# A scan inside groups of 8 tokens: a tree up and down around the levels over groups, for serial steps and a wide product

## The chip, the cores and the metric

The kernel runs on one core of a Trainium2 chip. The metric is device time in microseconds of one execution; a comparison is made from several executions of each kernel on the same chip. The clock that the profile grants TensorE is given as a share of its higher level (1.00 is 2.4 GHz, 0.50 is 1.2 GHz).

## What is computed

A linear attention with a complex decay, then two feed-forward layers. Cut to what matters:

```python
# q, k, v, a_re, a_im: (4, 8, 768, 48) float32
mag = sqrt(a_re**2 + a_im**2)
a = (a_re + 1j * a_im) * minimum(mag, 0.999) / (mag + 1e-6)
for t in range(768):                       # per batch and head
    S = a[t][:, None] * S + outer(k[t], v[t])
    y[t] = q[t] @ S.real
x = y.transpose(0, 2, 1, 3).reshape(3072, 384)
h = maximum(x @ w_in, 0);  x = (h * h) @ w_out        # 384 -> 2048 -> 384
h = x @ w2_in;  out = (h * sigmoid(1.702 * h)) @ w2_out
```

The kernel doesn't step through t. Inside a stretch of tokens it needs the running products of the decays a from the stretch's start, for every token; q is multiplied by them and k by their inverse, and the rest is matrix products with a causal mask.

## The kernel before

**Units and chunks.** The 3072 tokens are cut into twelve units of 256 tokens (three per batch), and each unit into two chunks of 128. A unit's tokens lie in 32 groups of J = 8 consecutive tokens. In the tile `ab` of a unit (128 partitions x 2 x 8 x 96) the two planes c are the real and the imaginary part, j is the token within its group of 8, and the last axis is 3 blocks of 32 groups.

**What a unit does, in order.** `normalize(u)` (line 414) loads the decays, transposes them (line 405) and scales them (up to line 448). `scan(u)` (line 454) makes the running products: first seven serial steps over j, each multiplying plane j by plane j-1 (one multiply into `mm`, line 467, and a difference and a sum, lines 471 and 473); after them plane 7 holds the product of each group. Then five levels over the 32 groups of plane 7 (lines 491 and 495, doubling the stretch each time) make running products of groups. ScalarE copies these, shifted by one group, to `eexc` with a 1 ahead of each block, and their negated imaginary part (lines 505 and 506). At last planes 0 to 6 are multiplied by the product of all groups before theirs, in two halves of four and three planes: two multiplies and a sum each (lines 514 and 518). Behind the scan, q and k are multiplied (lines 529 and 571), written to `scr` in device memory (lines 535 and 585), and read back with heads turned as `qs` (line 599; for the first two chunks half of the loads are issued on ScalarE's queue).

**What a chunk does.** `chunk` (line 621) makes scores on TensorE (`pa`, line 638), masks them on GpSimd (`asb`, line 642), multiplies them by v (`px`), and carries the state. Its result is the input `xh`, `xl` of the first layer.

**The layers.** Work on the layers comes in jobs: twelve of 256 tokens for the first, then eight of 384 for the second, each of sixteen steps m over the 2048 hidden columns. A step has a first product (`h`, line 837) and a second (`acc`, lines 882 and 884). Weights arrive as packed words: `decode` (line 738) loads one to a `raw` buffer (of three, line 742), and ScalarE (lines 750, 753) and VectorE (lines 755, 756, 758) make `wf` of it; `split` (line 764) makes a high and a low part (line 779 on ScalarE, line 780 on VectorE) for the three-term products. Job 0 uses unsplit first weights and jobs 0 to 2 unsplit second ones. `wf`, high and low parts live in a ring `w` of 66 slots; for the first eight steps of the second layer, high and low parts live in the buffers that the attention no longer needs. A job's end is three evictions (`o`, line 894) and stores to `x2d` (line 895).

**What sets the order.** All of this is first noted as operations with an engine, an assumed duration, the buffers that they read and write, and due times. `Plan` then simulates the engines: at each moment it gives an engine the operation that can start earliest, and among those the most urgent, so an engine whose urgent operation isn't ready takes any other that is. It does this forty times, moving due times earlier where TensorE stood idle, and emits the order with the earliest end. Each engine, and SyncE's queue of loads, then runs its list in that order. Buffers are rings: the next buffer of a ring is given out in the order of the program and only when a slot is free.

Of the kernel before, what the change touches and what calls it, by code (L numbers as in the profile page):

```python
# [24 lines left out]
J = 8  # L25
# [9 lines left out]
BLAME = 1.5  # L35

# [24 lines left out]

class Op:
    __slots__ = ("eng", "ns", "lat", "fn", "due", "prio", "pred", "raw", "succ", "bufs", "wait", "start", "end", "idx", "ready", "port", "fresh")


class Plan:
# [5 lines left out]
    PORT = ()  # L72
    AHEAD = {"PE": 0, "DVE": 0, "ACT": 0, "POOL": 0, "SP": 0}
# [13 lines left out]
    def op(self, eng, ns, fn, r=(), w=(), lat=None, due=1e12, port=True):  # L87
        o = Op()
        o.eng, o.ns, o.fn, o.due, o.port = eng, float(ns), fn, due, port and eng in self.PORT
# [52 lines left out]
    def forward(self):  # L142
# [15 lines left out]
        order, freed, held = [], [], dict.fromkeys(self.PORT, 0.0)  # L158
# [20 lines left out]
        while len(order) < len(ops):  # L179
            best = None  # L180
            for e in sorted(cand, key=free.get):
# [4 lines left out]
                for o in os:  # L186
                    t = earliest(o)
                    if t is None:
                        continue
                    t = max(t, f)  # L190
                    if o.port:
                        t = max(t, held["POOL" if e == "DVE" else "DVE"])
                    can.append((t, o.prio, o.idx, o))
# [3 lines left out]
                urgent = min((c for c in can if c[0] <= pick[0] + self.AHEAD[e]), key=lambda c: c[1:3])  # L197
# [10 lines left out]
            if o.port:  # L208
                held[o.eng] = t + o.ns
# [37 lines left out]
def fast(ctx: ExitStack, tc: tile.TileContext, q, k, v, a_re, a_im, w1, w2, out, flag):  # L247
# [47 lines left out]
    ring("m", 1)  # L295
# [7 lines left out]
    ring("w", 4 * NF + 2)  # L303
# [35 lines left out]
    eexc = const.tile([128, 3, 3, 32], F32, name="eexc")  # L339
# [4 lines left out]
    def setup():  # L344
        def consts():
            P.memset(tiny, 2.0 ** -56)
            P.memset(shb, SH * math.log(2.0))
            P.memset(eexc, 0.0)
            P.memset(eexc[:, 0, :, 0:1], 1.0)
# [10 lines left out]
        op("POOL", 800, consts, w=["consts", "eexc", "eexm"])  # L360
# [42 lines left out]
    def tr(u, dst, nm, w):  # L403
        t = nat_t.pop((u, nm))
        op("DVE", ve(96 * groups(u)), lambda: V.transpose(out=f(dst()), in_=t().rearrange("p h j d -> p j h d")), r=[t], w=w, port=False)
# [5 lines left out]
    def planes(ab, js, cs=(0, 1)):  # L411
        return [(ab, c, j) for c in cs for j in range(js.start, js.stop)]

    def normalize(u):
        J = groups(u)
        ab = ab_t[u] = buf("ab", [128, 2, J, 96], name="ab")
# [37 lines left out]
    def scan(u):  # L454
        J, CPU = groups(u), count(u)
        HJ, U = (J + 1) // 2, 32 * J
        ab = ab_t.pop(u)
        load_nat(u, "q", q)
        load_nat(u, "k", k)

        for j in range(1, J):
            m = buf("mm", [128, 2, 2, 96], name="mm")

            def go(j=j, m=m):
                x = ab()[:, :, j - 1].unsqueeze(1).to_broadcast([128, 2, 2, 96])
                y = ab()[:, :, j].unsqueeze(2).to_broadcast([128, 2, 2, 96])
                V.tensor_tensor(m(), x, y, ALU.mult)  # L467

            js = slice(j, j + 1)
            op("DVE", ve(384), go, r=planes(ab, slice(j - 1, j + 1)), w=[m])  # L470
            op("DVE", ve(96), lambda j=j, m=m: V.tensor_tensor(ab()[:, 0, j], m()[:, 0, 0], m()[:, 1, 1], ALU.subtract),
               r=[m], w=planes(ab, js, (0,)))
            op("DVE", ve(96), lambda j=j, m=m: V.tensor_tensor(ab()[:, 1, j], m()[:, 0, 1], m()[:, 1, 0], ALU.add),
               r=[m], w=planes(ab, js, (1,)))
# [3 lines left out]
        while h < 32:  # L478
# [10 lines left out]
            def times(c, parts=parts):  # L489
# [7 lines left out]
            for c in range(2):  # L497
                op("DVE", ve(96), lambda c=c, times=times: times(c), r=lastp, w=[(m, c)])
# [5 lines left out]
        g = lambda: ab()[:, :, J - 1].rearrange("p c (x r) -> p c x r", r=32)  # L504
        op("ACT", 240, lambda: A.copy(eexc[:, 0:2, :, 1:32], g()[:, :, :, 0:31]), r=lastp, w=["eexc"])
        op("ACT", 170, lambda: A.mul(eexc[:, 2, :, 1:32], g()[:, 1, :, 0:31], -1.0), r=[lastp[1]], w=["eexm"])
# [655 lines left out]
```

## Time and profile before

| | before |
|---|---|
| runs, median of 3 | 1070.24 us (1068.86 to 1072.58) |
| profiled execution | 1070.3 us |
| its span, first to last instruction | 1068.6 us |
| TensorE busy | 968.2 us |
| VectorE busy | 751.9 us |
| ScalarE busy | 608.3 us |
| GpSimd busy | 48.6 us |

Time outside the span is 1.7 us. In the rows below PE is TensorE (PEld its weight loads), DVE is VectorE, ACT is ScalarE, POOL is GpSimd and SP is SyncE; a q behind a name is the engine's queue, as it issues transfers. L467 is line 467 of the kernel. `out<-in` are tile names, and x is a count.

### The profile page before, as it was taken

The numbers are of one execution on the slowest core, as the hardware profiler recorded it, in microseconds if no ns is written. First come the engines' busy times: TensorE is split into PE (matmuls) and PEld (weight loads), VectorE is DVE, ScalarE is ACT, GpSimd is POOL, SyncE is SP. The second block draws the span as 40 slices with busy tenths as digits, with TensorE's granted clock in tenths as the row PEclk, the third lists the DMA queues.
The fourth block names the chain that finished last, engine by engine and source line by source line (L and its number), as shares of the span: only waits on it lengthen the run. The fifth ranks groups of instructions, "written<-read, shape, count | busy, mean of one in ns | idle before, by whom it ended". The sixth has DMA issues, their size and how long they took to land.

```text
span 1068.6 us, 20733 instructions
## 1 busy us (share of the span) xinstructions
PE 968.2 (91%) x7858; PEld 937.7 (88%) x7858; DVE 751.9 (70%) x1514; ACT 608.3 (57%) x1506; POOL 48.6 (5%) x70
## 2 busy tenths in 40 slices
PE   0029899999999999999999999999999999999996
PEld 0028789898999999999999999999999999999996
DVE  6979899899988899998899678843434333333332
ACT  4527587558576666758676799643434333333332
POOL 1000000000101011010100100000000000000000
PEclk9999999999999999999999999999999999999999
DMA  7586867366473637355552754110101010100000
GB/s 206 153 195 164 191 162 144 90 134 146 100 168 81 158 79 142 99 119 142 104 127 62 168 189 141 60 46 1 45 1 45 1 45 4 42 1 23 9 15 26
DMA packets 133486, 102.28 MB, mean 96 GB/s; under 512 B 46848, under 2 KB 125184, under 8 KB 133376
## 3 DMA queue, kind: packets, MB, share of 16 engines
q1 hardware_dynamic: 132000, 99.47, 39.2%
q10 hardware_dynamic: 1376, 1.38, 0.5%
q8 instruction: 64, 1.05, 0.4%
q14 instruction: 46, 0.38, 0.1%
HBM read 72.43 MB, written 28.39 MB: 94 GB/s over the span
## 4 chain that ended last, share of the span: by engine, by line
PE 57%; DVE 22%; DMA 8%; ACT 8%; issue 4%; SPq 1%; DVEq 0%; ACTq 0%
PE h L837 27%; PE acc L884 19%; PE acc L882 10%; DMA x2d<-o 3%; DVE mm L491 2%; DMA raw<-in_w_dram 2%; DVE mm L467 2%; DVE ab L495 2%; DVE gl L852 2%; DVE ab L514 1%; DVE ab L518 1%; DVE wf L756 1%; DVE m L514 1%; DVE wf L758 1%; PE pa L638 1%
## 5 line engine op out<-in xcount | busy, mean ns | idle before, releaser
L852 DVE TENSOR_TENSOR gl<-g,gh 128x256 fp32r<-128x256 f32 (+1 forms) x272 | 132.2, 489 | 96.9 <-ACT gh L851 73.4
L846 DVE TENSOR_TENSOR g<-g,h 128x384 f32<-128x384 f32 x128 | 70.8, 553 | 146.7 <-ACT g L845 146.6
L851 ACT CAST gh<-g 128x256 fp32r<-128x256 f32 (+1 forms) x272 | 124.2, 458 | 78.0 <-DVE g L846 75.2
L845 ACT ACTIVATE g<-h 128x384 f32<-128x384 f32 x128 | 62.9, 491 | 158.8 <-PE h L837 158.8
L837 PE MATMUL h<-xh,wh 128*128 128x256 f32 (+1 forms) x720 | 140.1, 303 | 2.3 <-ACT xh L697 1.1
L837 PE MATMUL h<-xh,wl 128*128 128x256 f32 (+1 forms) x720 | 134.6, 295 | 0.1
L837 PE MATMUL h<-xl,wh 128*128 128x256 f32 (+1 forms) x720 | 134.2, 296 | 0.0
L638 PE MATMUL pa<-qs 96*128 96x128 f32 x384 | 50.6, 285 | 75.1 <-DMA qs<-scr 73.6
L837 PEld LDWEIGHTS h<-xh,wh 128*128 128x128 f32 x720 | 109.4, 188 | 6.6 <-ACT g L842 3.6
L638 PEld LDWEIGHTS pa<-qs 96*128 96x128 f32 x384 | 47.0, 197 | 76.0 <-issue 73.5
L837 PEld LDWEIGHTS h<-xl,wh 128*128 128x128 f32 x720 | 107.9, 188 | 1.7 <-issue 1.1
L842 ACT ACTIVATE g<-h 128x256 f32<-128x256 f32 x192 | 72.8, 382 | 64.2 <-PE h L837 61.2
L837 PEld LDWEIGHTS h<-xh,wl 128*128 128x128 f32 x720 | 108.5, 188 | 0.8 <-DVE wl L780 0.5
L882 PE MATMUL acc<-gh,wh 128*128 128x256 f32 x432 | 80.9, 282 | 7.6 <-ACT o L894 7.5
L843 ACT ACTIVATE g<-g 128x256 f32<-128x256 f32 x192 | 80.0, 420 | 3.5
L882 PE MATMUL acc<-gl,wh 128*128 128x256 f32 x432 | 80.8, 282 | 0.4 <-DVE gl L852 0.2
L884 PE MATMUL acc<-w,gh 128*128 128x384 f32 x384 | 79.7, 336 | 0.0
L882 PE MATMUL acc<-gh,wl 128*128 128x256 f32 x432 | 79.5, 279 | 0.0
L837 PE MATMUL h<-xh,w 128*128 128x384 f32 x384 | 77.7, 337 | 0.1
L882 PEld LDWEIGHTS acc<-gh,wh 128*128 128x128 f32 x432 | 63.1, 189 | 10.1 <-ACT o L894 8.9
L642 POOL TENSOR_SCALAR_AFFINE_SELECT asb<-asb 128x512 f32<-128x512 f32 x48 | 45.2, 950 | 565.8 <-ACT asb L646 565.3
L882 PE MATMUL acc<-g,wf 128*128 128x256 f32 x288 | 69.2, 380 | 0.0
(122 smaller groups left out, 1936.2 us busy)
## 6 DMA issues: line engine op xcount, KB each, us to landing
raw<-in_w_dram SPq DMA_DIRECT2D x64, 384.0 KB
scr<-tq SPq DMA_DIRECT2D x24, 384.0 KB
qs<-scr SPq DMA_DIRECT2D x46, 129.0 KB
qs<-scr SPq DMA_DIRECT2D x46, 128.0 KB
scr<-tk SPq DMA_DIRECT2D x12, 390.0 KB
nat_k<-in_k_dram SPq DMA_DIRECT2D x48, 96.0 KB
scr<-tk SPq DMA_DIRECT2D x12, 384.0 KB
x2d<-o SPq DMA_DIRECT2D x36, 128.0 KB
```

The lines of the kernel that those rows point to most:

```text
L467: V.tensor_tensor(m(), x, y, ALU.mult)
L638: T.matmul(pa()[:, h], lhsT=qs()[:, 4 * g + h, kcol], rhs=qs()[:, 4 * g + h, qcol], start=True, stop=True)
L642: P.affine_select(out=tj, in_=tj, pattern=[[0, 4], [1, J], [J, C // J]], base=0, channel_multiplier=-1, compare_op=ALU.is_ge, fill=0.0)
L837: T.matmul(h()[:, :n], lhsT=ww()[:, kk * 128:kk * 128 + 128], rhs=xx()[:, kk, :n], start=(i == kk == 0), stop=(i == len(terms) - 1 and kk ...
L842: op("ACT", ac(n) - 30, lambda: A.activation(g()[:, :n], h()[:, :n], AF.Relu), r=[h], w=[g])
L843: op("ACT", ac(n), lambda: A.activation(g()[:, :n], g()[:, :n], AF.Square), r=[g], w=[g])
L845: op("ACT", ac(n) - 30, lambda: A.activation(g()[:, :n], h()[:, :n], AF.Sigmoid, scale=1.702), r=[h], w=[g])
L846: op("DVE", ve(n), lambda: V.tensor_tensor(g()[:, :n], g()[:, :n], h()[:, :n], ALU.mult), r=[h, g], w=[g], port=False)
L851: op("ACT", ac(n), lambda: A.copy(gh()[:, :n], g()[:, :n]), r=[g], w=[gh])
L852: op("DVE", ve(n), lambda: V.tensor_tensor(gl()[:, :n], g()[:, :n], gh()[:, :n].bitcast(F32), ALU.subtract), r=[g, gh], w=[gl])
L882: T.matmul(acc[i]()[:, :n], lhsT=ww()[:, i * 128:i * 128 + 128], rhs=gg()[:, :n], **st_)
L884: T.matmul(acc[i](), lhsT=gg()[:, i * 128:i * 128 + 128], rhs=ww(), **st_)
```

## The change

Within a group of 8 tokens the seven serial steps and the wide product are replaced by one tree. The tile gains a plane in front (index 0), so a token's plane j is now index j+1. On the way up, products of neighbours are made for 4, then 2, then 1 planes at once, so that index 8 holds the group's product. The five levels over the 32 groups stay. ScalarE then copies index 8, shifted by one group, to index 0, with a 1 ahead of each block. On the way down, for 1, then 2, then 4 planes at once, a plane is multiplied by the one half a stretch before it. Each such call is two multiplies (one per plane c), a difference and a sum.

`mm` grows from 384 elements per partition to 1536, `ab` by a ninth, the ring `m` goes, and `w` has 65 slots instead of 66. The other edits change nothing that runs: `port`, `PORT` and `held` were empty, and `FILL` and `HOLD` with `HOLD = 0` leave the look-ahead at nought.

```diff
-    ring("m", 1)
-    ring("w", 4 * NF + 2)
+    ring("w", 4 * NF + 1)
-    eexc = const.tile([128, 3, 3, 32], F32, name="eexc")
+    ones2 = const.tile([128, 6], F32, name="ones2")
...
-        ab = ab_t[u] = buf("ab", [128, 2, J, 96], name="ab")
+        full = ab_t[u] = buf("ab", [128, 2, J + 1, 96], name="ab")
+        ab = Part(full, lambda t: t[:, :, 1:])
...
-        for j in range(1, J):
-            m = buf("mm", [128, 2, 2, 96], name="mm")
-            def go(j=j, m=m):
-                x = ab()[:, :, j - 1].unsqueeze(1).to_broadcast([128, 2, 2, 96])
-                y = ab()[:, :, j].unsqueeze(2).to_broadcast([128, 2, 2, 96])
-                V.tensor_tensor(m(), x, y, ALU.mult)
-            js = slice(j, j + 1)
-            op("DVE", ve(384), go, r=planes(ab, slice(j - 1, j + 1)), w=[m])
-            op("DVE", ve(96), lambda j=j, m=m: V.tensor_tensor(ab()[:, 0, j], m()[:, 0, 0], m()[:, 1, 1], ALU.subtract), ...
-            op("DVE", ve(96), lambda j=j, m=m: V.tensor_tensor(ab()[:, 1, j], m()[:, 0, 1], m()[:, 1, 0], ALU.add), ...
+        def times(x, y, n, step):
+            m = buf("mm", [128, 2, 2, n, 96], name="mm")
+            at = lambda k: slice(k, k + (n - 1) * step + 1, step)
+            xs = [(full, c, x + i * step - 1) for c in range(2) for i in range(n)]
+            ys = [[(full, c, y + i * step - 1) for i in range(n)] for c in range(2)]
+            def part(c):
+                V.tensor_tensor(m()[:, c], full()[:, :, at(x)],
+                                full()[:, c:c + 1, at(y)].to_broadcast([128, 2, n, 96]), ALU.mult)
+            for c in range(2):
+                op("DVE", ve(192 * n), lambda c=c: part(c), r=[*xs, *ys[c]], w=[(m, c)])
+            op("DVE", ve(96 * n), lambda: V.tensor_tensor(full()[:, 0, at(y)], m()[:, 0, 0], m()[:, 1, 1], ALU.subtract),
+               r=[(m, 0), (m, 1)], w=ys[0])
+            op("DVE", ve(96 * n), lambda: V.tensor_tensor(full()[:, 1, at(y)], m()[:, 0, 1], m()[:, 1, 0], ALU.add),
+               r=[(m, 0), (m, 1)], w=ys[1])
+        n = J // 2
+        while n:
+            times(J // (2 * n), J // n, n, J // n)
+            n //= 2
...
-        op("ACT", 240, lambda: A.copy(eexc[:, 0:2, :, 1:32], g()[:, :, :, 0:31]), r=lastp, w=["eexc"])
-        op("ACT", 170, lambda: A.mul(eexc[:, 2, :, 1:32], g()[:, 1, :, 0:31], -1.0), r=[lastp[1]], w=["eexm"])
-        ee = eexc.rearrange("p c x r -> p c (x r)")
-        for js in (slice(0, HJ), slice(HJ, J - 1)) if J > 4 else (slice(0, J - 1),):
...
-            op("DVE", ve(192 * n), lambda p2=p2, n=n, mul=mul: mul(p2()[:, :, :n], 1), ...
-            op("DVE", ve(192 * n), lambda js=js, mul=mul: mul(ab()[:, :, js], 0), ...
-            op("DVE", ve(192 * n), lambda p2=p2, js=js, n=n: V.tensor_tensor(
-                ab()[:, :, js], ab()[:, :, js], p2()[:, ::-1, :n], ALU.add), ...
+        def before():
+            g = full().rearrange("p c j (x r) -> p c j x r", r=32)
+            A.copy(g[:, :, 0, :, 1:32], g[:, :, J, :, 0:31])
+        op("ACT", 75, lambda: A.copy(full().rearrange("p c j (x r) -> p c j x r", r=32)[:, :, 0, :, 0],
+                                     ones2.rearrange("p (c x) -> p c x", c=2)), r=["ones2", *lastp], w=[(full, "one")])
+        op("ACT", 240, before, r=[*lastp, (full, "one")], w=first)
+        n = 1
+        while n < J:
+            times(0, J // (2 * n), n, J // n)
+            n *= 2
```

## Rows read from the trace of the kernel before

**Rows 1.** The page's first part: busy us, share of the span, instructions.
```profile
PE 968.2 (91%) x7858; PEld 937.7 (88%) x7858; DVE 751.9 (70%) x1514; ACT 608.3 (57%) x1506; POOL 48.6 (5%) x70
```
**Rows 2.** Busy time by stage: stretch, length, then PE, PEld, DVE, ACT, POOL; clock, DMA.
```profile
0.00:59.00 59.00, 0.00 (x0) 0.00 (x0) 48.90 (x103) 30.38 (x72) 3.40 (x22) 1.00 0.63 174
59.00:88.00 29.00, 14.20 (x177) 12.65 (x178) 22.93 (x62) 9.98 (x27) 3.34 (x4) 1.00 0.90 210
...
133.00:657.00 524.00, 510.21 (x5165) 488.08 (x5158) 472.12 (x962) 379.41 (x995) 39.97 (x42) 1.00 0.56 127
657.00:1068.60 411.60, 402.77 (x2311) 401.84 (x2310) 167.57 (x316) 159.98 (x337) 0.00 (x0) 1.00 0.10 29
```
**Rows 3.** What PE waited for: us in total, times, longest us.
```profile
PE pa L638 <- DMA qs<-scr: 73.6, 3, 72.6
PE acc L882 <- ACT o L894: 7.5, 5, 2.0
...
PE px L671 <- POOL asb L642: 0.5, 2, 0.4
```
**Rows 4.** DVE in order of time, unit 0's serial steps: start us, us, instruction.
```profile
21.98 0.52 DVE L467 TENSOR_TENSOR mm<-ab 128x384 f32<-128x384 f32 x1
22.53 0.26 DVE L471 TENSOR_TENSOR ab<-mm 128x96 f32<-128x96 f32 x1
22.71 0.25 DVE L473 TENSOR_TENSOR ab<-mm 128x96 f32<-128x96 f32 x1
...
25.94 0.55 DVE L467 TENSOR_TENSOR mm<-ab 128x384 f32<-128x384 f32 x1
26.41 0.35 DVE L755 TENSOR_SCALAR wf<-wf 128x384 int32<-128x384 int32 x1
...
31.98 0.25 DVE L473 TENSOR_TENSOR ab<-mm 128x96 f32<-128x96 f32 x1
```
**Rows 5.** DVE in order of time, first and last instruction of unit 0's wide product.
```profile
39.92 0.95 DVE L514 TENSOR_TENSOR m<-ab,eexc 128x768 f32<-128x768 f32 x1
...
45.19 0.75 DVE L518 TENSOR_TENSOR ab<-ab,m 128x576 f32<-128x576 f32 x1
```
**Rows 6.** ACT by line: count, busy us, mean ns, idle before and its releaser.
```profile
L505 ACT COPY eexc<-ab 128x186 f32<-128x186 f32 x12 | 4.1, 346 | 10.6 <-DVE ab L495 10.6
L506 ACT ACTIVATE eexc<-ab 128x93 f32<-128x93 f32 x12 | 3.3, 274 | 0.0
```
**Rows 7.** All engines in order of time, from the first reload to the first scores.
```profile
62.24 8.36 ACTq L599 DMA_DIRECT2D qs<-scr  x8
67.07 0.35 SPq L742 DMA_DIRECT2D raw<-in_w_dram  x1
...
72.63 0.77 PE L638 MATMUL pa<-qs 96*128 96x128 f32 x2 [72.63 <-DMA qs<-scr]
...
73.98 0.55 PE L638 MATMUL pa<-qs 96*128 96x128 f32 x1 [0.58 <-DMA qs<-scr]
```
**Rows 8.** PE in order of time: a wait in job 0, the second layer's first product.
```profile
122.78 1.65 PE L837 MATMUL h<-xh,wf 128*128 128x256 f32 x3 [3.27 <-DVE wf L758]
...
654.80 1.20 PE L837 MATMUL h<-xh,w 128*128 128x384 f32 x6
```
**Rows 9.** All engines in order of time: two masks and two multiplies.
```profile
83.34 1.65 POOL L642 TENSOR_SCALAR_AFFINE_SELECT asb<-asb 128x512 f32<-128x512 f32 x2 [4.50 <-ACT asb L646]
83.39 1.67 DVE L491 TENSOR_TENSOR mm<-ab 128x96 f32<-128x96 f32 x2
```
**Rows 10.** DVE in order of time, four of the splits of the second layer's weights.
```profile
592.09 0.55 DVE L780 TENSOR_TENSOR w<-wf,w 128x384 fp32r<-128x384 f32 x1
...
597.86 0.55 DVE L780 TENSOR_TENSOR w<-wf,w 128x384 fp32r<-128x384 f32 x1
...
621.57 0.55 DVE L780 TENSOR_TENSOR w<-wf,w 128x384 fp32r<-128x384 f32 x1
...
690.25 0.56 DVE L780 TENSOR_TENSOR wl<-wf,wh 128x384 fp32r<-128x384 f32 x1
```

More of the change, by code (lines that the diff above doesn't have):

```diff
@@ L35 @@
 BLAME = 1.5
+FILL = 55e3
+HOLD = 0
 def _limit_pair():
@@ L59, in __call__, with __init__ @@
         return self.tile
+class Part:
+    def __init__(self, buf, cut):
+        self.buf, self.cut = buf, cut
+    def __call__(self):
+        return self.cut(self.buf())
 class Op:
-    __slots__ = ("eng", "ns", "lat", "fn", "due", "prio", "pred", "raw", "succ", "bufs", "wait", "start", "end", "idx", "ready", "port", "fresh")
+    __slots__ = ("eng", "ns", "lat", "fn", "due", "prio", "pred", "raw", "succ", "bufs", "wait", "start", "end", "idx", "ready", "fresh")
 class Plan:
     LAT = {"PE": 260, "DVE": 160, "ACT": 170, "POOL": 160, "SP": 0}
-    PORT = ()
-    AHEAD = {"PE": 0, "DVE": 0, "ACT": 0, "POOL": 0, "SP": 0}
+    AHEAD = {"DVE": HOLD, "ACT": HOLD, "SP": HOLD}
     OWN = {"PE": 0, "DVE": 95, "ACT": 95, "POOL": 95, "SP": 0}
@@ L85, in buf, with op @@
         return b
-    def op(self, eng, ns, fn, r=(), w=(), lat=None, due=1e12, port=True):
+    def op(self, eng, ns, fn, r=(), w=(), lat=None, due=1e12):
         o = Op()
-        o.eng, o.ns, o.fn, o.due, o.port = eng, float(ns), fn, due, port and eng in self.PORT
+        o.eng, o.ns, o.fn, o.due = eng, float(ns), fn, due
         o.lat = self.LAT[eng] if lat is None else lat
@@ L157, in forward @@
                 cand[o.eng].append(o)
-        order, freed, held = [], [], dict.fromkeys(self.PORT, 0.0)
+        order, freed = [], []
         rank = {x: i for g in self.rings.values() for i, x in enumerate(g["order"])}
@@ L196, in forward @@
                 pick = min(can)
-                urgent = min((c for c in can if c[0] <= pick[0] + self.AHEAD[e]), key=lambda c: c[1:3])
+                ahead = self.AHEAD.get(e, 0) if pick[0] < FILL else 0
+                urgent = min((c for c in can if c[0] <= pick[0] + ahead), key=lambda c: c[1:3])
                 if urgent[0] > pick[0]:
@@ L404, in tr @@
         t = nat_t.pop((u, nm))
-        op("DVE", ve(96 * groups(u)), lambda: V.transpose(out=f(dst()), in_=t().rearrange("p h j d -> p j h d")), r=[t], w=w, port=False)
+        op("DVE", ve(96 * groups(u)), lambda: V.transpose(out=f(dst()), in_=t().rearrange("p h j d -> p j h d")), r=[t], w=w)
     def tmp(n):
@@ L411, in planes @@
     def planes(ab, js, cs=(0, 1)):
-        return [(ab, c, j) for c in cs for j in range(js.start, js.stop)]
+        return [(ab.buf, c, j) for c in cs for j in range(js.start, js.stop)]
     def normalize(u):
         J = groups(u)
-        ab = ab_t[u] = buf("ab", [128, 2, J, 96], name="ab")
+        full = ab_t[u] = buf("ab", [128, 2, J + 1, 96], name="ab")
+        ab = Part(full, lambda t: t[:, :, 1:])
         load_nat(u, "re", a_re)
@@ L487, in parts, with level @@
                 return sec, t, left
-            def times(c, parts=parts):
+            def level(c, parts=parts):
                 sec, t, left = parts()
@@ L497, in scan @@
             for c in range(2):
-                op("DVE", ve(96), lambda c=c, times=times: times(c), r=lastp, w=[(m, c)])
+                op("DVE", ve(96), lambda c=c, level=level: level(c), r=lastp, w=[(m, c)])
             for c in range(2):
@@ L700, in chunk @@
             op("DVE", ve(384), lambda: V.tensor_tensor(xl()[:, :, o:o + C], px(), xh()[:, :, o:o + C].bitcast(F32), ALU.subtract),
-               r=[px, (xh, o)], w=[(xl, o)], due=due, port=False)
+               r=[px, (xh, o)], w=[(xl, o)], due=due)
         if last:
```

37 lines of the change are left out of this document (11 added, 26 removed).

## The prediction

> **What bounds the kernel now.** I read the busy shares first. TensorE works 91% of the span [rows 1], which says nothing yet about order, so I cut the span into stages by what TensorE does [rows 2]. Before 59 us it does nothing while VectorE is busy 48.9 us of 59. From 133 to 657 us it is busy 510.2 of 524 us, and from 657 us on 402.8 of 411.6 us, with VectorE at 41% there. Then I asked what TensorE waits for [rows 3]: 73.6 us for reloads of `qs`, nearly all of it for the first chunk, 7.5 us over the whole run for evictions of the accumulators, and little else. So the kernel is a start-up of some 74 us and then TensorE's own work nearly end to end. A change is worth what it moves the first products forward, less what TensorE then waits more; time freed on VectorE after 133 us buys at most part of the 14 us that TensorE idles there.
>
> The start-up is the path of unit 0: normalise, scan, products, store and reload. The scan lies on VectorE from 21.98 us, where the first step over groups begins [rows 4], to 45.94 us, where the wide product ends [rows 5]. From there the order is unchanged.
>
> **The steps up.** Before: seven steps of one 384-element multiply and two 96-element sums, each step needing the one before. From one start to the next, a 384-element instruction takes 0.47 us when the next one doesn't need it (25.94 to 26.41) and 0.55 us when it does (21.98 to 22.53); a 96-element one takes 0.18 us (22.53 to 22.71) [rows 4]. That fits 0.08 us plus 1.0 ns per element. Seven steps by themselves are 7 x (0.47 + 2 x 0.18) = 5.8 us, but they lasted from 21.98 to 32.2 us, 10.2 us. The other 4.4 us are weight decoding (the `wf` line between two steps [rows 4]) that the planner's work-conserving choice puts into the dependent places, since a place that isn't ready at once goes to any ready instruction. There are 14 such places, so 0.31 us each.
>
> After: three levels of n = 4, 2, 1 products, each two multiplies of 192n and two sums of 96n elements. By the same fit 768, 384, 192 and 96 elements take 0.85, 0.47, 0.28 and 0.18 us, so the levels take 2 x (0.85 + 0.47) + 2 x (0.47 + 0.28) + 2 x (0.28 + 0.18) = 5.1 us. Elements are the same 4032; the instructions are 12 for 21. Dependent places are 6 (sum after multiplies, next level after sums): at 0.31 us, 1.9 us. Together 7.0 us, so 3.2 us less on the path.
>
> **The steps down.** Before: two independent halves of three wide instructions, lasting from 39.92 to 45.94 us, 6.0 us with some decoding between [rows 5]. After: the mirror of the way up, 5.1 us and 6 dependent places, 7.0 us; 1.0 us more on the path. Here the change loses, because the wide product had hardly any dependent places and the tree has one every two instructions. Net on unit 0's path: 2.2 us less. The bounds come from the price of a dependent place: if each costs only the 0.08 us by which 0.55 exceeds 0.47, the tree takes 2 x (5.1 + 0.5) = 11.2 us against 16.2, which is 5.0 us less; if each is filled by a whole 384-element decode at 0.47 us, it takes 15.8 us, 0.4 us less. I take 0.31, which is what this planner made of such places in this very stretch. That strided operands could run slower per element no row shows: the multiply before already reads two broadcast operands at 384 elements and keeps the fit.
>
> **The copy between them.** Two ScalarE copies, 346 and 274 ns [rows 6], become a copy of the same 186 elements and one of 6 elements in place of the one of 93. That can only be shorter, by at most the 274 ns; I put it at nothing.
>
> **What carries the gain to TensorE.** `qs` comes by eight loads issued on ScalarE from 62.24 us and eight on SyncE, the latter behind a weight load that SyncE could issue only at 67.07 us, when a `raw` buffer was free [rows 7]. The loads feed the first products at 72.63 and 73.98 us. The decoding that frees `raw` is what the tree displaces (three or four fewer fillers), so this weight load could stay where it was; it would hold back the second products by at most the 1.35 us between the two. From the landing on TensorE is nearly solid to 119.5 us, then waits 3.27 us for a weight [rows 8]. If decoding is no earlier, all of the 2.2 us reappears there; if everything before it moves along, nothing does. VectorE idles 6.1 us between 59 and 88 us [rows 2], waiting and not working, so most of the decoding can move along; I take 0.5 us back. Sum so far: -1.7 us.
>
> **After 133 us.** Per unit VectorE's own work falls by 0.24 us (27 instructions become 24, at 0.08 us each; the elements are the same) plus some four dependent places at 0.08 us; over eleven units some 3 to 6 us of a VectorE that has 52 us idle in that stage [rows 2]. TensorE doesn't wait on it there, so I count -0.3 us. A longer multiply also holds up what queues behind it: a 768-element one 0.38 us longer than a 384-element one. The wide product has 768-element instructions already [rows 5], so nothing; but the new order reshuffles the 7.5 us of eviction waits [rows 3], which are five places of some 1.5 us: bounds -4 to +4 us, value 0.
>
> One rule is to be weighed. When GpSimd masks scores, two 96-element multiplies into `mm`, 0.18 us each by the fit, last 1.67 us, as long as the two masks [rows 9]: the two engines exclude each other. The Trainium skill, "SBUF — State Buffer", section "SBUF: two separate sides", says that a VectorE instruction with two SBUF inputs and a GpSimd one take a shared port pair as an exclusive lock for the whole instruction. By that rule longer multiplies could also hold up the masks, which speaks against the change: up to 0.38 us more per mask. TensorE waits 0.5 us in all for masks [rows 3], so by row the sum stays as it is; by the rule it would be no more than 1 us worse.
>
> **The slot given up.** The larger buffers are paid with one `w` slot, 65 for 66. While the first layer's split weights hold 64, the second layer's decoding ahead of the last job of the first runs through two slots before and one after. A slot turns over in some 5.8 us: the split at 592.09 us frees the one that is split next at 597.86 us [rows 10]. From 592.09 to 621.57 us, when that last job begins to release weights, nine splits ran; through one slot it would be 29.5 / 5.8, some six with the first. The nineteen left to 690.25 us took 3.6 us each, so three late ones are 11 us. The second layer's products begin at 654.80 us [rows 8], and its eight jobs take 402.8 us [rows 2], 50.3 each and 3.15 for each of sixteen steps: the last step's weight is due at 654.8 + 15 x 3.15 = 702 us, 11 us after the last split ended. Cover and delay are equal, and weight loads already in flight catch some of it up: I take 0. If the cover is gone, each further late weight costs 3.6 us.
>
> **Sum.** -2.2 + 0.5 - 0.3 = -2.0 us. The profiled execution took 1070.3 us for a span of 1068.6 us, and the median of the runs is 1070.24 us, so the two scales agree and the forecast is 1068.3 us.
>
> **The rivals.**
> (a) The slot decides: the second layer starves. For it: one slot less where they are fewest, 11 us against 11. Against: nothing of what TensorE now waits for in that stage is a split, and the planner can move decoding forward. It decides from the point where the last splits fall behind 702 us; two weights further cost 2 x 3.6 us on the forecast, 1075 us, slower than before.
> (b) Weights pace: the 3.27 us wait takes all of the gain back, or the planner fills the tree's places as it filled the steps': 1070.3 us. For it: the wait exists, and the displaced decoding is done later. Against: VectorE's idle time before it.
> (c) The tree pays only the 0.08 us per place, because no decoding is ready at those moments (decoding hangs on weight loads): -5 us at the start, 1065 us.
> (d) The planner's new order is simply worse at the job changes, +4 us: 1074 us. That is also the case in which the change doesn't do what it says, since the whole order is planned anew and the tree is one input to it.
>
> **How the numbers follow.** A measurement here can tell 0.3%, 3.2 us, from no change, so faster means under 1067.0 and slower over 1073.5 us. The forecast case holds 0.45, with 0.15 of it under 1067.0; (a) 0.17; (b) 0.12; (c) 0.18; (d) 0.08. Faster: 0.15 + 0.18 = 0.33; same: 0.30 + 0.12 = 0.42; slower: 0.17 + 0.08 = 0.25. The range reaches from (c) with 3 us of better job changes, 1062 us, to (a) with two more microseconds, 1077 us. The likeliest case by itself spans 1065.5 to 1071 us.
>
> **What would show it.** Right: unit 0's way up ends near 29 us instead of 32.2, the way down takes about 7 us, the first scores start near 70.5 us, and TensorE's wait for a weight near 120 us stays under 4 us. Wrong: the first scores at 72.6 us or later; TensorE idle in the job that starts near 655 us with a split as releaser (a); a wait near 120 us that grows by as much as the start gained (b). A start that is earlier by 2 us and an end that is not would say that the time went to the job changes (d). The forecast falls altogether if TensorE's idle time after 133 us changes by more than the start does.

## The result and the profile after

| | before | after |
|---|---|---|
| median of the runs compared | 1069.55 us | 1054.85 us (1052.93 to 1058.94) |
| ratio after to before | | 0.9883, 95% interval 0.9861 to 0.9904 |
| profiled execution | 1070.3 us | 1054.74 us |
| its span | 1068.6 us | 1052.7 us |

The forecast of 1068.3 us was wrong, and so was its range (1062 to 1077 us): the change is faster by 1.2%. In microseconds that is 12.5 by the ratio (10.3 to 14.9 by its interval), 14.7 by the medians and 15.6 by the two profiled executions, whose stages are compared below. Executions of one kernel differ by several microseconds (20 of before on one chip took 1064.2 to 1073.2 us), so a stage read from one execution of each kernel is good to a few microseconds only. The first part of the page of after answers [rows 1], and its stretches, read in the same way, answer [rows 2] (the last one begins where the first layer ends, at 648.4 us):

```profile
PE 961.8 (91%) x7858; PEld 935.7 (89%) x7858; DVE 742.6 (71%) x1478; ACT 607.9 (58%) x1506; POOL 54.1 (5%) x70
```

```profile
0.00:59.00 59.00, 0.00 (x0) 0.00 (x0) 49.32 (x101) 30.35 (x72) 3.16 (x22) 1.00 0.66 177
59.00:88.00 29.00, 17.20 (x192) 15.38 (x193) 25.16 (x65) 11.44 (x32) 3.52 (x4) 1.00 0.90 212
133.00:657.00 524.00, 514.16 (x5109) 496.14 (x5110) 471.57 (x953) 387.29 (x1014) 42.69 (x40) 1.00 0.56 129
648.40:1052.70 404.30, 395.49 (x2264) 394.82 (x2264) 158.81 (x297) 151.18 (x316) 0.00 (x0) 0.99 0.08 24
```

The busy shares have hardly moved (TensorE 91% before and after), though 16 us are gone. They don't say where; a table by stage does. A stage ends where the third eviction of a job begins (the third copy `o` of an accumulator, line 894 before and 909 after):

| stage | before | after | difference |
|---|---|---|---|
| start to first scores | 72.6 | 69.5 | -3.1 |
| job 0 | 80.9 | 76.3 | -4.6 |
| jobs 1 to 11 | 509.8 | 502.6 | -7.2 |
| second layer and tail | 405.3 | 404.3 | -1.0 |

The same stretches by busy time, job 0 and jobs 1 to 11, first of before, then of after (length, PE, PEld, DVE, ACT, POOL, clock, DMA):

```profile
72.60:153.50 80.90, 75.66 (x619) 66.24 (x620) 72.46 (x164) 54.06 (x148) 7.42 (x8) 0.98 0.79 186
153.50:663.30 509.80, 495.99 (x4971) 475.47 (x4970) 456.29 (x918) 368.94 (x963) 37.73 (x40) 1.00 0.55 124
```

```profile
69.50:145.80 76.30, 73.09 (x620) 64.76 (x621) 71.13 (x162) 55.53 (x151) 8.23 (x8) 1.00 0.81 201
145.80:648.40 502.60, 493.20 (x4977) 476.07 (x4975) 452.81 (x899) 370.86 (x968) 42.69 (x40) 1.00 0.56 128
```

In jobs 1 to 11 the weight loads (PEld) are busy for the same time, 475.5 and 476.1 us, as the same work should be. What changed are the gaps between them: 509.8 - 475.5 = 34.3 us before, 26.5 us after. The matmul column shows gaps of 13.8 and 9.4 us only; its ends are modelled by the profiler, which may hide short waits.

What TensorE waits for, after, beside [rows 3] (us in total, times, longest us):

```profile
PE pa L653 <- DMA qs<-scr: 69.9, 2, 69.5
PE h L852 <- ACT g L857: 2.7, 2, 2.3
PE h L852 <- DVE wf L773: 1.9, 2, 1.5
PE px L686 <- POOL asb L657: 1.6, 4, 0.8
PE acc L897 <- ACT o L909: 1.3, 2, 1.0
PE acc L899 <- ACT o L909: 1.2, 1, 1.2
```

Waits for evictions (`o`) fell from 7.5 us to 2.5 us, 1.2 us of which lie at the change to the second layer (line 899). One more wait belongs with them in after, although it bears another name. ScalarE's third eviction at 244.41 us waits 2.64 us for a store, the operation `g` stands behind that eviction on ScalarE, and TensorE waits 2.27 us for `g`:

```profile
244.41 0.37 ACT L909 COPY o<-acc 128x256 f32<-128x256 f32 x1 [2.64 <-DMA x2d<-o]
244.68 0.39 ACT L857 ACTIVATE g<-h 128x256 f32<-128x256 f32 x1
```

```profile
245.12 0.97 PE L852 MATMUL h<-xh,wh 128*128 128x256 f32 x3 [2.27 <-ACT g L857]
```

Counted with it, what TensorE waits behind an eviction fell from 7.5 to 4.8 us. Nothing in the tree touches an eviction. That is what the experiments had to explain.

The start went much as forecast. Unit 0's scan on VectorE after, in order of time (start us, us, instruction), to be laid beside [rows 4, 5]:

```profile
21.99 1.78 DVE L478 TENSOR_TENSOR mm<-ab 128x768 f32<-128x768 f32 x2
23.69 0.35 DVE L770 TENSOR_SCALAR wf<-wf 128x384 int32<-128x384 int32 x1
23.95 0.55 DVE L483 TENSOR_TENSOR ab<-mm 128x384 f32<-128x384 f32 x1
...
28.75 0.25 DVE L485 TENSOR_TENSOR ab<-mm 128x96 f32<-128x96 f32 x1
...
37.16 0.62 DVE L478 TENSOR_TENSOR mm<-ab 128x192 f32<-128x192 f32 x2
...
43.66 0.55 DVE L485 TENSOR_TENSOR ab<-mm 128x384 f32<-128x384 f32 x1
```

The way up takes 21.99 to 29.0 us, the way down 37.16 to 44.1 us, 7.0 us each, decoding in dependent places included (the `wf` line is one of five on the way up). The five levels between them took 8.2 us for 7.7, so the scan ends 1.8 us earlier than before. The reloads then gained 1.3 us more, to be read beside [rows 7]:

```profile
60.78 5.78 ACTq L614 DMA_DIRECT2D qs<-scr  x8
64.91 5.49 SPq L614 DMA_DIRECT2D qs<-scr  x8
69.51 0.77 PE L653 MATMUL pa<-qs 96*128 96x128 f32 x2 [69.51 <-DMA qs<-scr]
```

No weight load stands ahead of SyncE's eight any more, and ScalarE issues its eight in 5.8 us for 8.4.

### The profile page after: what moved, and what is told of

Its sections match the earlier page's. It is cut to its first block, busy times and chain, and to the rows that moved or that the text cites. A ratio compares the mean times of both kernels' runs of the same rounds, so it can differ in the third digit from the quotient of the medians.

```text
span 1052.7 us, 20660 instructions
## 1 busy us (share of the span) xinstructions
PE 961.8 (91%) x7858; PEld 935.7 (89%) x7858; DVE 742.6 (71%) x1478; ACT 607.9 (58%) x1506; POOL 54.1 (5%) x70
## 4 chain that ended last, share of the span: by engine, by line
PE 72%; ACT 9%; DVE 8%; DMA 8%; issue 2%; SPq 1%; POOL 0%; ACTq 0%; DVEq 0%
PE h L852 31%; PE acc L899 19%; PE acc L897 13%; PE pa L653 3%; DMA raw<-in_w_dram 2%; DMA x2d<-o 2%; PE pt L723 2%; DVE mm L478 2%; DMA v<-in_v_dram 1%; ACT wf L768 1%; ACT g L858 1%; ACT raw L765 1%; DMA qs<-scr 1%; ACT g L857 1%; DVE wf L773 1%
## 5 line engine op out<-in xcount | busy, mean ns | idle before, releaser
L857 ACT ACTIVATE g<-h 128x256 f32<-128x256 f32 x192 | 73.1, 381 | 72.7 <-PE h L852 70.5
L653 PE MATMUL pa<-qs 96*128 96x128 f32 x384 | 50.5, 284 | 70.6 <-DMA qs<-scr 69.9
L653 PEld LDWEIGHTS pa<-qs 96*128 96x128 f32 x384 | 46.9, 197 | 71.6 <-DMA qs<-scr 69.5
L478 DVE TENSOR_TENSOR mm<-ab 128x384 f32<-128x384 f32 (+2 forms) x144 | 89.3, 655 | 2.9 <-ACT ab L526 2.0
L657 POOL TENSOR_SCALAR_AFFINE_SELECT asb<-asb 128x512 f32<-128x512 f32 x48 | 50.9, 1072 | 543.0 <-ACT asb L661 542.6
L899 PEld LDWEIGHTS acc<-w,gh 128*128 128x128 f32 x384 | 67.9, 188 | 1.6 <-ACT o L909 1.5
```

Source lines behind the costliest of these rows:

```text
L478: V.tensor_tensor(m()[:, c], full()[:, :, at(x)], full()[:, c:c + 1, at(y)].to_broadcast([128, 2, n, 96]), ALU.mult)
L653: T.matmul(pa()[:, h], lhsT=qs()[:, 4 * g + h, kcol], rhs=qs()[:, 4 * g + h, qcol], start=True, stop=True)
L657: P.affine_select(out=tj, in_=tj, pattern=[[0, 4], [1, J], [J, C // J]], base=0, channel_multiplier=-1, compare_op=ALU.is_ge, fill=0.0)
L857: op("ACT", ac(n) - 30, lambda: A.activation(g()[:, :n], h()[:, :n], AF.Relu), r=[h], w=[g])
L899: T.matmul(acc[i](), lhsT=gg()[:, i * 128:i * 128 + 128], rhs=ww(), **st_)
```

## Theories

The prediction had left 13 us unexplained, and three theories could supply them. The tree's own work: fewer dependent places in all twelve units, not only in the first. The slot: 65 slots for split weights order the decoding better than 66. The draw of the order: the planner makes a new order of thousands of operations, and any edit, however neutral, may move the time by as much. All ratios below are to the kernel before on the same chip, with a 95% interval; after's is 0.9883 (0.9861 to 0.9904).

## Experiments: the slot, the work and the order apart

**serial_65.** Before with the slot alone given up.

```diff
-    ring("w", 4 * NF + 2)
+    ring("w", 4 * NF + 1)
```

> The kernel before with 65 slots of w instead of 66 and nothing else; the planner draws its order anew. Theory A (the tree's shorter chain of dependent instructions earns the 15 us) and theory B (the new order around the scan earns it, the tree itself only some 3 us at the start): 1062 to 1076 us here, since neither the tree nor its order is in it. Theory C (the slot: one early decoded weight less leaves loads and ScalarE freer in the middle): 1050 to 1060 us, and then the tree has little to do with it. The prediction's rival (a), that the slot starves the second layer, would show here alone as 1073 us or more with splits as releasers after 650 us.

Measured: 0.9916 (0.9876 to 0.9956), 1059.0 us by the median. That lies in theory C's range and under that of theories A and B. A slot less, with the new order that it brings, makes the kernel faster, which the prediction had taken as a possible loss only.

**tree_in_serial_order and steps_in_tree_order.** Two crossed kernels. In the first, the order planned for serial_65 is kept (the planner sees the seven steps and the wide product with their durations), and the places of their 27 instructions are filled with the tree's 24. In the second, the order of after is kept and its 24 places are filled with the steps and the wide product. One operation of each edit is shown; the others are filled in the same way.

```diff
...
-            op("DVE", ve(384), go, r=planes(ab, slice(j - 1, j + 1)), w=[m])
+            op("DVE", ve(384), next(ups), r=planes(ab, slice(j - 1, j + 1)), w=[m])
...
```

```diff
...
-                op("DVE", ve(192 * n), lambda c=c: part(c), r=[*xs, *ys[c]], w=[(m, c)])
+                op("DVE", ve(192 * n), next(slots), r=[*xs, *ys[c]], w=[(m, c)])
...
```

In steps_in_tree_order the last instruction of the wide product stands where the tree's last sum stood, behind some of its readers, so that part of planes 4 to 6 is read before it is complete; the instructions and their number are those of before.

> The order that the planner makes for the serial steps with 65 slots is kept, instruction by instruction on every engine; only in the places of the 21 step instructions stand the 12 of the way up, and in the 6 of the wide product the 12 of the way down. So work changes and order doesn't. Theory A: the tree brings its gain here too, 8 to 15 us less than the serial kernel with 65 slots. Theory B: within 4 us of the serial kernel with 65 slots; the start may be up to 1 us earlier, as VectorE's list is 0.24 us per unit shorter and has fewer dependent places.

> The mirror: the order that the planner makes for the tree, with the 21 step instructions in the 12 places of the way up and the 6 wide ones in the 12 places of the way down. Theory A: the gain goes, 1062 to 1070 us. Theory B: the gain stays but for what VectorE's dependent steps cost at the start: 1053 to 1060 us, first scores at 69.5 to 71 us, job ends as in the changed kernel to 3 us.

Measured: 0.9974 (0.9952 to 0.9995) and 1.0055 (1.0037 to 1.0073). With after and serial_65 they make a square, from one profiled execution each (us):

| | first scores | jobs 1 to 11 |
|---|---|---|
| steps, their own order (serial_65) | 74.8 | 502.2 |
| tree, in the steps' order | 72.9 | 505.2 |
| steps, in the tree's order | 70.9 | 517.9 |
| tree, its own order (after) | 69.5 | 502.6 |

The tree's work by itself brings the first scores forward by 1.4 to 1.9 us, in either order; the prediction's 2.2 us was of that size. The order made for the tree brings 3.4 to 3.9 us more, reckoned from serial_65, whose first scores come 2.2 us later than before's. The profiled execution of serial_65 took 1065.6 us and is the slowest of five (median 1059.0), so one of its stages may stand up to 6.6 us too high.

In the jobs neither work gains in the other's order: a fixed order fits the durations for which it was planned, and when they are others 3.0 us are lost with the tree in the steps' order and 15.3 us with the steps in the tree's. Neither theory had forecast this. Theory A wanted tree_in_serial_order 8 to 15 us under serial_65, and by the medians it is 5.7 us over it; theory B wanted steps_in_tree_order at 1053 to 1060 us, and it took 1074.5, more than theory A's 1070 too. So the tree's instructions by themselves don't explain the jobs, and the theory of its own work falls as the explanation of the whole gain. The crossed kernels can't price the two orders against each other, since each order is made for one work only.

## Experiments: the draw of the order

Edits that change nothing of the work but make the planner find another order: due times of the attention 1 us later (LEAD), a step of the due times larger (BLAME), and one pass of planning for forty (PASSES). Each is made on before, on after, and two of them on serial_65.

```diff
-LEAD = 12e3
+LEAD = 11e3
```

```diff
-BLAME = 1.5
+BLAME = 1.6
```

```diff
-PASSES = 40
+PASSES = 1
```

> The kernel before with one constant of its planner changed: the results of a chunk are due 11 us instead of 12 us ahead of their job. The work is the same; only the order is drawn anew. Theory D (a new draw of the order moves the time by several us whatever the work, and the 15 us are a lucky draw on top of some 3 us at the start): 1058 to 1075 us, more than 3 us away from the kernel before. Theory A (the tree's work earns the 15 us, order matters little): within 3 us of the kernel before, 1064 to 1071 us.

> The kernel before with another constant of its planner: a gap of TensorE makes the operation behind it more urgent by 1.6 instead of 1.5 times its length. Theory D: 1058 to 1075 us, and not the same as with the other constant. Theory A: within 3 us of the kernel before.

> The kernel before with the planner's first order taken as it is (one pass, no due times moved by gaps). Theory C (with 66 slots the scan falls on the job ends, where the stores of the evictions meet the loads of the next unit, whatever the pass): jobs 1 to 11 take 508 to 518 us from the end of job 0 to that of job 11, with 6 to 9 us of waits for evictions; 1068 to 1080 us. Theory E (the passes bring it about, the slot is a bystander): 500 to 506 us, as with 65 slots.

> Serial steps, 65 slots, results of a chunk due 11 us ahead: the pair to the run with 66 slots and the same constant, 1.005 of the kernel before. Theory C: 0.988 to 0.996 of the kernel before, jobs 1 to 11 in 500 to 506 us. Theory D (draws scatter whatever the slot): anywhere from 0.99 to 1.01.

> The same with 65 slots. Theory C: jobs 1 to 11 take 500 to 506 us with under 3 us of waits for evictions, 1058 to 1066 us, 8 us or more under the first pass with 66 slots. Theory E: within 3 us of the first pass with 66 slots.

> The changed kernel with the results of a chunk due 11 us ahead. Theory A: 1052 to 1058 us, as the changed kernel. Theory D: anywhere from 1052 to 1068 us; the start (first scores at 69 to 71 us) stays, the rest is drawn anew.

> The changed kernel with the factor 1.6 in its planner. Theory A: 1052 to 1058 us. Theory D: anywhere from 1052 to 1068 us, with the first scores at 69 to 71 us. If both tree draws and both serial draws stay with their kernels, D falls; if they overlap, A falls as the whole cause.

> The changed kernel with one pass. If the tree's own part is the start alone (theory C with the tree worth some 3 us): first scores at 69 to 71 us, jobs 1 to 11 in 500 to 506 us, 3 to 5 us under the first pass of the serial steps with 65 slots. If the tree shortens the middle too (theory A): jobs 1 to 11 under 500 us and 8 us or more under it.

Measured, with TensorE's waits for evictions, the time of the first scores and the length of jobs 1 to 11 from the profile of each (us); 66 and 65 are slots:

| kernel | ratio | interval | waits for evictions | first scores | jobs 1 to 11 |
|---|---|---|---|---|---|
| serial_lead11 (66) | 1.0053 | 1.0030 to 1.0075 | 10.2 | 73.4 | 515.6 |
| before (66) | 1 | | 7.5 | 72.6 | 509.8 |
| serial_blame16 (66) | 0.9997 | 0.9977 to 1.0017 | 8.7 | 74.1 | 511.0 |
| serial65_lead11 | 0.9961 | 0.9939 to 0.9984 | 6.1 | 73.0 | 508.4 |
| serial66_pass1 | 0.9948 | 0.9923 to 0.9974 | 0.0 | 73.3 | 507.5 |
| serial65_pass1 | 0.9937 | 0.9917 to 0.9957 | 0.4 | 73.4 | 505.2 |
| serial_65 | 0.9916 | 0.9876 to 0.9956 | 1.3 | 74.8 | 502.2 |
| tree_blame16 (65) | 0.9878 | 0.9837 to 0.9918 | 3.2 | 70.5 | 502.3 |
| tree_pass1 (65) | 0.9867 | 0.9828 to 0.9905 | 3.3 | 69.9 | 503.5 |
| tree_lead11 (65) | 0.9860 | 0.9832 to 0.9887 | 4.9 | 70.5 | 501.1 |

Three things follow. The draw alone moves a serial kernel by 1%, from 0.9948 to 1.0053 at 66 slots. It doesn't explain the tree: all four orders of the tree, after's among them, lie at 0.986 to 0.988, under every serial one (of the halved tree below, one of two lies at 0.9911, level with serial_65). The closest pair is the one with a single pass and 65 slots, on the same chip: 1066.7 us with the steps and 1058.7 with the tree, 8 us where 3 to 5 were expected, of which 1.7 us lie in jobs 1 to 11. And the serial kernels fall into two sets by their waits for evictions. The four with 6 us and more have a mean ratio of 1.0003 and 511.2 us for jobs 1 to 11; the three others, with 0 to 1.3 us, 0.9934 and 505.0 us. The set with more slots isn't the slow set: serial66_pass1 has no such wait, serial65_lead11 has 6.1 us and misses the 500 to 506 us that theory C wanted of it. (The 507.5 us of serial66_pass1 hold 10.2 us at half the clock, some 5 us lost; without them it would lie near 502.) So the slot is not what separates them, and the place to look at is an eviction.

## Experiments: what an eviction waits for

A job's end in before, SyncE's queue, then the evictions on ScalarE and the product behind them (start us, us):

```profile
482.92 1.22 SPq L535 DMA_DIRECT2D scr<-tq  x2
484.23 0.84 SPq L895 DMA_DIRECT2D x2d<-o  x1
485.17 2.56 SPq L396 DMA_DIRECT2D nat_re<-in_a_re_dram  x4
487.82 3.10 SPq L895 DMA_DIRECT2D x2d<-o  x2
```

```profile
483.31 0.64 ACT L894 COPY o<-acc 128x256 f32<-128x256 f32 x2
490.19 0.37 ACT L894 COPY o<-acc 128x256 f32<-128x256 f32 x1 [1.29 <-DMA x2d<-o]
```

```profile
490.61 0.38 PE L882 MATMUL acc<-gh,wh 128*128 128x256 f32 x1 [1.64 <-ACT o L894]
```

There are two buffers `o` for three evictions, so the third needs the first one's store to have landed. That store was issued at 484.23 us, behind two stores of `scr` of 384 KB each, and had landed at 490.19 us, 6.0 us later. Four loads of the next decays were issued behind it, and the second store of the job behind them. ScalarE waits 1.29 us, TensorE 1.64 us. The planner reckons with 3 us for the landing and gives the store no due time of its own (line 895). All five waits of before [rows 3], near 302, 350, 490, 535 and 583 us, have this form on SyncE's queue: two stores of `scr` right ahead of the first store, and loads of decays or of `v` between the stores of the job. The third eviction begins 6.5 to 7.4 us after the second there, and 2.3 to 4.4 us after it at the seven other jobs' ends.

**serial66_store_due and tree_store_due.** The store gets a due time, in before and in after.

```diff
-                       w=[("x2d", i, t) for t in range(t0, t0 + n, C)], lat=3000)
+                       w=[("x2d", i, t) for t in range(t0, t0 + n, C)], lat=3000, due=due + 1500)
```

> The kernel before, with a due time for the store of the first layer's result (the one of the second product plus 1.5 us) where it had none. If the order of stores behind loads on SyncE's queue is what makes the third eviction of a job wait (a store at 484.2 us, then loads of the decays, the other two stores only at 487.8 us), TensorE's waits for evictions fall from 7.5 us to under 3 us and the time by 4 to 7 us, ratio 0.993 to 0.997. If the waits are only an accident of the whole order, they come out anywhere between 0 and 9 us and the ratio within 0.995 to 1.005. If the loads that the stores now pass were needed as soon, first scores or masks of the next unit wait instead, ratio over 1.000.

> The changed kernel with the same due time for the store. Its TensorE waits 1.3 us for evictions and 1.2 us for accumulators, so by the theory of the store order there are at most 2.5 us to win: ratio 0.986 to 0.989 to the kernel before. If planning anew moves the time by itself, anywhere in 0.983 to 0.993.

Measured: 0.9930 (0.9910 to 0.9950) for the serial kernel, 0.9878 (0.9848 to 0.9908) for the tree. The serial kernel's waits for evictions, its jobs 1 to 11, and the same job's end:

```profile
PE acc L882 <- ACT o L894: 1.6, 3, 0.7
```

```profile
156.40:660.70 504.30, 494.35 (x4987) 476.17 (x4988) 456.83 (x921) 371.66 (x972) 39.59 (x40) 1.00 0.56 126
```

```profile
481.15 1.22 SPq L535 DMA_DIRECT2D scr<-tq  x2
483.24 2.21 SPq L396 DMA_DIRECT2D nat_re<-in_a_re_dram  x4
485.98 5.12 SPq L895 DMA_DIRECT2D x2d<-o  x3
```

```profile
485.60 0.67 ACT L894 COPY o<-acc 128x256 f32<-128x256 f32 x2
490.38 0.38 ACT L894 COPY o<-acc 128x256 f32<-128x256 f32 x1
```

The third eviction waits for nothing there, and neither does TensorE. The waits fall by 5.9 us, jobs 1 to 11 by 5.5 us (509.8 to 504.3), the gaps between weight loads from 34.3 to 28.1 us, and the kernel by 0.7%, with the steps and the 66 slots still in it and the first scores 2.4 us later than in before. Some 1.7 of the 5.5 us are the clock: in before it drops behind the wait of 1.97 us that ends at 350.40 us, and in this kernel it drops nowhere in these jobs.

```profile
351.40:354.70 3.30, 3.30 (x17) 3.30 (x17) 3.30 (x5) 1.38 (x5) 0.00 (x0) 0.50 0.07 25
```

So by this pair an order without these waits is worth 5 to 8 us. That the due time brings it about is less certain, since with it the whole order is drawn anew, and this is one draw. Nor did it act as meant at the job's end shown: the loads still go first, and all three stores behind them. What is gone is the pair of `scr` stores right ahead of the first store; it now lies 4.8 us ahead.

All kept traces can tell which neighbour matters. The 17 kernels have twelve such job ends each; a store of `scr` counts as right ahead if it was issued less than 2 us before the job's first store:

| ahead of and behind the first store | job ends | ScalarE's third eviction waits for the store |
|---|---|---|
| stores of `scr` right ahead | 30 | at all 30, 1.2 to 3.2 us |
| none right ahead, loads of decays or `v` behind | 65 | at 5, 0.4 to 0.9 us |
| neither | 109 | at 23, 0.3 to 2.1 us |

The first store had landed 5.0 to 6.8 us after its issue at the 30. So the stores ahead mark the wait, and loads behind by themselves don't; that the stores would do it alone isn't shown, since all 30 have loads behind as well. Such job ends number three to five in the four serial kernels with 6 us of waits and more, none in the other serial ones (serial66_store_due among them), two in after and in each of its four redrawn orders, none and two in the crossed kernels, and none and one in the halved trees that follow. Why the due time won nothing in the tree, where 2.7 us of waits for evictions stay and the ratio is no better than after's, can be read at one of its two. It put two of the job's stores ahead of all loads, and the wait on ScalarE is 2.89 us all the same:

```profile
239.69 1.22 SPq L550 DMA_DIRECT2D scr<-tq  x2
241.00 2.05 SPq L910 DMA_DIRECT2D x2d<-o  x2
243.17 1.98 SPq L403 DMA_DIRECT2D nat_re<-in_a_re_dram  x4
```

```profile
247.64 0.37 ACT L909 COPY o<-acc 128x256 f32<-128x256 f32 x1 [2.89 <-DMA x2d<-o]
```

No run keeps these two kinds of store apart on purpose, and none has a third buffer `o`, which might take the wait away by another road.

The two kernels with the due time also compare tree and steps on one chip, with none of these job ends in the steps and two in the tree: 1060.4 us against 1066.5 us, 6 us (some 2 to 9 by the intervals of the ratios). By their profiles it lies in the first scores (75.0 to 70.7 us) and job 0 (81.4 to 78.2 us); jobs 1 to 11 last 504.3 and 504.4 us.

**treeh_66 and treeh_65.** The tree's widest level in two calls of two planes, so that `mm` is half as large and 66 slots fit; the second with 65.

```diff
-            times(J // (2 * n), J // n, n, J // n)
+            for i in range(0, n, 2):
+                times(J // (2 * n) + i * (J // n), J // n + i * (J // n), min(n, 2), J // n)
...
-            times(0, J // (2 * n), n, J // n)
+            for i in range(0, n, 2):
+                times(i * (J // n), J // (2 * n) + i * (J // n), min(n, 2), J // n)
```

> The tree with its widest level made in two calls of two planes, so that the temporary is half as large and 66 slots for split weights fit. If the slot given up is a part of the gain by itself, this stands 0.3% to 0.9% above the next kernel, ratio 0.991 to 0.997. If the tree alone earns the whole 1.2%, both stand at 0.986 to 0.990. Either way the first scores start near 70 us, 2.5 to 3.5 us ahead of the kernel before.

> The same with 65 slots. Eight more instructions per unit than the tree's 24 at 0.08 us each, some 0.6 us on the first unit's path: ratio 0.987 to 0.991, whichever theory of the slot holds. If the draw of the order decides by itself, as much as 0.4% away from that.

Measured: 0.9863 (0.9829 to 0.9897) with 66 slots, 0.9911 (0.9881 to 0.9941) with 65. The slot given up was worth 0.8%, 0.1% and 0.9% in the three pairs of serial kernels (before and serial_65, one pass, LEAD) and is worth -0.5% here, from four runs each with intervals that overlap. With that the theory of the slot falls: what it is worth changes with the order, and perhaps its sign. Waits for evictions are 0 with 66 slots and 2.1 us with 65; first scores come at 70.5 and 70.7 us, as in every tree.

## Why the prediction was wrong, point by point

**After 133 us: the step that failed.** This term was put at -0.3 us, because TensorE doesn't wait for VectorE there, and the eviction waits in it were given the value 0 with bounds of -4 to +4 us, as if a new order were as likely to lengthen as to shorten them. Jobs 1 to 11 became 7.2 us shorter. The waits that bear the name of an eviction fell by 5.0 us, outside those bounds, and by 2.7 us, inside them, with the wait for `g` counted in; the rest lies in short gaps between weight loads that no run put down to a cause. The eviction waits were seen [rows 3] and called five places of some 1.5 us. One look at SyncE's queue at the five would have shown one form five times over, a result's store right behind two stores of `scr`, and so that an order without it could give all 7.5 us back at once. Rival (d), a new order that decides at the job changes, had the right place with the sign turned: before was already at the bad end. The prediction's own last sign came true: TensorE's idle time after the start changed by more (4.4 us by the matmuls of jobs 1 to 11) than the start did (3.1 us).

**What bounds the kernel.** That the kernel is "then TensorE's own work nearly end to end" was read from the matmul column of [rows 2], where 14 us are idle. The column beside it, the weight loads, stood at 488.1 of 524 us in the same row: 36 us of gaps. The Trainium skill, "Perfetto Trace Analysis", section "Identifying the Most-Contended Engine", says that matmul occupancy is a poor measure of how near the limit TensorE is, and that the busy share of the weight loads is one of two good ones. The traces agree: over jobs 1 to 11 the weight loads' gaps changed by 7.8 us while the length changed by 7.2 us, and the matmuls' gaps by 4.4 us. The 7.2 us would have fitted into the 14 us too, so this reading helped the small value along and does not explain it alone.

**The steps up and down.** Right: 7.0 us each were forecast and measured. The net on unit 0's scan was 1.8 us for 2.2, the 0.4 us being given back in the five levels between.

**What carries the gain to TensorE.** First scores moved by 3.1 us, not 2.2. By the square the tree's work by itself makes 1.4 to 1.9 us, and the order that was made for it the rest. The weight load that "could stay where it was" ahead of SyncE's reloads did not stay.

**The wait for a weight in job 0.** +0.5 us was forecast; job 0 became 4.6 us shorter. Of that, 1.8 us are the wait itself, 3.27 us before [rows 8] and 1.45 us after:

```profile
132.98 1.56 PE L852 MATMUL h<-xh,wf 128*128 128x256 f32 x6 [1.45 <-DVE wf L773]
```

Some 1.6 us are what followed it in before, where the clock had dropped:

```profile
122.80:126.20 3.40, 3.40 (x9) 2.75 (x10) 3.40 (x10) 0.43 (x2) 0.00 (x0) 0.53 1.06 210
```

The other 1.2 us were not traced. This term is not the tree's alone, and a gain of 4.6 us is in part a lucky draw: over all orders of the tree, the halved ones among them, job 0 lasts 76.3 to 86.6 us, over the serial ones 80.9 to 83.0 us.

**The slot.** That it might starve the second layer, rival (a), falls: from the first layer's end on, after takes 404.3 us, before 405.3 us, and no split is waited for there; the one new wait is the 1.2 us at its start for the first layer's last eviction. That it costs nothing held; that it could only cost was the mistake, since planning anew is part of any such edit.

**Masks.** Waits for them rose from 0.5 us [rows 3] to 1.6 us, about the 1 us that was put beside the rule on the shared port. GpSimd is busy 54.1 us for 48.6, but serial66_pass1, without the tree, also shows more than before (42.9 us in jobs 1 to 11, where before has 37.7 and after 42.7), so no run shows that the longer multiplies do it.

**The other rivals.** (b), weights that pace, falls with the shorter wait in job 0. (c), cheaper dependent places, falls: the places were filled as forecast, 7.0 us up and down for the 5.6 us each that it wanted, and the whole lay 10 us under its 1065 us for other reasons.

**What the change is worth, then.** The parts can be priced along one road only: from before to serial66_store_due 0.7% (7 to 8 us), from there to tree_store_due 0.5% (6 us), which is about after's ratio. By that road about half of the gain is the tree, at the start and in job 0, and about half is the meeting of stores in before's order, which the new plan has at two job ends for five. The second half is luck as far as the tree goes, and it is an estimate: the due time redraws the order as well, and read straight from the traces of before and after the waits account for 2.7 us only. Why the orders of the tree have fewer such job ends is open: seven show 0 to 4.9 us of waits for evictions, serial ones 0 to 10.2 us, and nothing tried here separates chance from cause.

## What to carry to other kernels

Read how near TensorE is to its limit from the weight loads' column, and count the gaps there before calling a stage full. Where several waits of one size recur at one kind of place, look at the queue at one of them, and at what stands ahead of the transfer as well as behind it: a common cause gives all of them back at once, here in an order that is worth about as much as a rewritten scan. Follow a wait past its name: a wait for `g` can be one for the eviction ahead of it on the same engine, and so one for a store. Where a planner orders everything, time some neutral edits of both kernels before a difference of 1% is put down to an edit.

## What the runs showed of the chip

After TensorE had stood idle, the granted clock fell to the lower of its two levels for a while although work was there. In before, after the wait of 3.27 us, the six products from 122.78 us took 2.93 us, at a clock of 0.53 over the stretch shown above; the same six took 1.56 us in after at 132.98 us. That wait so cost almost half as much again as it lasted. In the profiled execution of treeh_66 a wait of 1.67 us for a mask, at 84.05 us, and another of 0.43 us stand ahead of a longer stretch:

```profile
85.00:95.20 10.20, 10.07 (x75) 8.60 (x76) 7.05 (x20) 4.17 (x13) 0.08 (x1) 0.50 0.30 72
```

10.2 us at half the clock are some 5 us lost, and job 0 lasted 86.6 us there for 82.1 in treeh_65. Serial kernels show such stretches too (serial66_pass1 one of 10.2 us near 200 us), so they are no property of the tree. And a store of 128 KB whose issue stood less than 2 us behind stores of `scr` (384 or 390 KB each) on the same queue landed 5.0 to 6.8 us after its own issue, at 30 job ends; with none of them right ahead, at 146 of 174 job ends the third eviction, most often some 4 us behind the first store's issue, did not wait for it.
